# A linear-attention layer and a top-2 expert layer in one kernel: a new order of the attention's work on four engines

## The chip, the cores and the metric

One core of a Trainium2 chip. The metric is device time in microseconds for one launch, the median of several runs; lower is better.

## The reference, cut to what matters

The first half is a recurrence over 768 time steps for 4 x 8 heads with a 40 x 40 state each; the second half routes each of 3072 rows of 320 to two of eight experts.

```python
for t in range(S):                                   # S = 768, D = 40
    y[:, :, t] = np.einsum('bhd,bhde->bhe', rt, state)
    Sa = np.einsum('bhde,bhe->bhd', state, at)
    state_decay = state * wt[:, :, None, :] - np.einsum('bhd,bhe->bhde', Sa, bt)
    state = state_decay + np.einsum('bhd,bhe->bhde', vt, kt)
...
logits = x @ w_gate                                  # x: y as (3072, 320)
noisy_logits = logits + np.log1p(np.exp(x @ w_noise)) * noise
top2 = np.argpartition(-noisy_logits, 2, axis=1)[:, :2]   # weights: softmax of the two
...
h = np.maximum(x[mask] @ w1[e], 0.0)                 # e = 0..7, F = 1024
out[mask] += top2_w[mask, k, None] * (h @ w2[e])
```

## The kernel before

**Units.** The sequence is cut into 12 chunks of 64 steps, and the 32 heads into two halves; a *unit* u (0 to 23) is one chunk of one half, 16 heads, so that u and u+2 are consecutive chunks of the same heads and share the state `S[u%2]`. Inside a unit the recurrence is done with matmuls: decays are multiplied into the inputs, a 64 x 64 triangular system per head is inverted, and the state is carried to the next chunk.

**What is done for a unit.** `scans` (L471) makes the cumulative decays with two scans on VectorE, `B` (L474) and `wq` (L478). `prods` (L479) multiplies them into k, b (`kb`, one GpSimd instruction of 1024 columns, L483) and a (`a`, L484). `LS` (L485) makes the triangular blocks on TensorE and copies them to `lab`. For four units at a time, `xtr` and `xmask` turn the blocks round, `solve` (L503) inverts 32 x 32 triangles column by column (j = 1 to 30, two tensor-tensor operations of j(31-j) elements for each), and `tout` (L510) transposes the result into `rp` and `dg`. `TA` and `TB` (L514, L523) build the 64 x 64 inverses from them. Then, in order: `W2`, `AK`, `U`, `UT`, `KBT`, `W1`, `P`, `dS`, `Y`, `RL` and `ST`, each some 16 to 32 small float32 matmuls (the profile counts each twice) and one copy or product out of PSUM. `P`'s product with the mask is `pm` (L612), `AK`'s is `akm` (L540); `dS` (L580) adds the unit's part to the state in two VectorE operations (L593, L594); `Y` (L613) makes the output, `xT` (L627) scales it; `RL` (L628) brings it back to rows and gives the routing's logits.

**Order.** Everything up to the experts is issued in the order of the program on each engine (`run`, L641). Step n of that loop works on several units at once: Y and RL of n-1, the middle part of n, AK, KBT, W1 and ST of n+1, scans, products and LS of n+8, and the solve for the next group of four units. With q = n mod 4, GpSimd does columns 1 to 13 of the solve in steps q = 0 and 1, VectorE columns 14 to 30 in q = 2, `tout` follows in q = 3, and TA and TB are done for two units at a time in q = 3 and q = 0. PSUM tiles come from a pool of three double banks (`p2`) and one of two banks (`p1`), each in rotation. `warm` (L450) issues matmuls of zeros into a tile ahead of the real ones.

**Routing.** After units 7, 15, 19, 21 and 23 `routed` (L108) runs `route` (L121) as a whole: the gate, the two largest logits, the positions in the experts' lists (with matmuls for running counts). `scatter` (L152) then writes list entries with indirect DMAs from GpSimd, so many in each step (L673), and `turn` (L115) copies the lists once, after unit 19. `zero` (L97) clears the output in steps 8 to 11. **Transfers** of the inputs are issued by the sync engine: `load` (L454) for the unit n+9, `load2` (L464) for n+2.

**Experts.** After the attention, eight experts run one after the other with split float16 matmuls (L277, L291). Their order is made by a planner.

Of the kernel before, what the change touches and what calls it, by code (L numbers as in the profile page):

```python
# [21 lines left out]
NA=20  # L22
# [20 lines left out]
class Moe:  # L43
    def __init__(s,nc,tc,ctx,aps):
        s.nc,s.tc=nc,tc
        s.wgn_d,s.nz_d,s.w1_d,s.w2_d,s.out_d=aps
        ec=ctx.enter_context
        s.kp=ec(tc.tile_pool(name="mk",bufs=1))
        s.rp=ec(tc.tile_pool(name="mr",bufs=MRB))
        s.dp=ec(tc.tile_pool(name="md",bufs=1,space=DRAM))  # L50
        s.scat=[]; s.half=0; s.parts=PARTS; s.cap=CAP; s.rts=list(RTS); s.todo=[]
        s.consts()
# [50 lines left out]
    def logit(s,n):  # L103

        if n==0: s.n0=0
        if n==s.n0: s.lg=s.rp.tile([128,RT,16],F32,name="lg")
        return s.lg[:,n-s.n0]
    def routed(s,n,ps,tag,bufs):  # L108

        if n-s.n0!=s.rts[0]-1: return  # L110
        s.route(s.n0,s.rts.pop(0),ps,tag,bufs)
        if n<NA: s.nc.sync.dma_start(s.xd[1][128*s.n0:128*n+128].rearrange("(p a) f->p (a f)",p=128),s.xd[0][128*s.n0:128*n+128].rearrange("(p a) f->p (a f)",p=128))
        s.n0=n+1
        if n+1==NA: s.turn()
# [6 lines left out]
    def route(s,n0,T,ps,tag,bufs):  # L121
# [4 lines left out]
        oh=s.gate(lg,s.nz[:,n0:n0+T],T,w[:,:,0],w[:,:,1])  # L126
# [3 lines left out]
        cnt=r("cnt",dt=F16); nc.vector.tensor_tensor(cnt,oh[:,:,0],oh[:,:,1],op=ALU.add)  # L130
        pr=ps.tile([128,T,8],F32,name="pr",tag=tag,bufs=bufs)
# [5 lines left out]
        for j in range(T): nc.gpsimd.tensor_tensor(h,p,cnt[:,j],op=ALU.add); p=h  # L137
        s.cumh=h
        rk=r("rk",(1,8))
# [11 lines left out]
        if n0+T>=NA: s.scatter(len(s.todo))  # L151
    def scatter(s,n):  # L152
# [8 lines left out]
    def gate(s,lg,nzt,T,w0,w1):  # L161
# [4 lines left out]
        u=r("u"); nc.scalar.activation(u,zc,AF.Exp)  # L166
        w=r("w"); nc.vector.tensor_scalar(w,u,1.0,None,op0=ALU.add)
        L=r("L_"); nc.scalar.activation(L,w,AF.Ln)
        iv=r("iv"); nc.scalar.activation(iv,L,AF.Exp,scale=-1.0)
        d=r("d"); nc.vector.scalar_tensor_tensor(d,w,1.0,u,op0=ALU.subtract,op1=ALU.subtract)  # L170
# [6 lines left out]
        nc.vector.tensor_tensor(z,z,lg[:,:,0:8],op=ALU.add)  # L177
        l12=r("l12")
# [6 lines left out]
        nc.scalar.activation(q[:,:,1],q[:,:,0],AF.Exp)  # L185
        nc.vector.tensor_scalar(q[:,:,2],q[:,:,1],1.0,1e-9,op0=ALU.add,op1=ALU.add)
# [189 lines left out]
NW,NAB,NKB=LP+3,LP+2,LP+1  # L376
RF=104

# [10 lines left out]
def host_att(inp):  # L389
# [12 lines left out]
            'iw':np.ascontiguousarray(iw.reshape(2,40,256)),'vt':np.ascontiguousarray(v.reshape(NU,2,64,320)),'pad':pad}  # L402

class Att:
    P2=3; P1=2
    def __init__(s,nc,tc,ctx,A,m):
# [10 lines left out]
        s.rb=[t([128,8,64],F32,name=f"rb{i}") for i in range(3)]  # L417
        s.vt=[t([128,8,64],F32,name=f"vt{i}") for i in range(2)]
        s.vu=[t([128,2,8,40],F32,name=f"vu{i}") for i in range(3)]
# [7 lines left out]
        s.tt={}; s.akm={}; s.pm={}; s.W={}; s.ut={}  # L427
# [36 lines left out]
    def load2(s,u):  # L464
        nc=s.nc
        for n,sl in (('gr',s.r),('gv',s.vt),('grb',s.rb)):
            z=s.fl(sl[u%len(sl)]); s.pads(z,u,sl)
            for y in range(2): nc.sync.dma_start(z[64*y:64*y+48],s.A[n][u,y])
        z=s.vu[u%3]
        for b in range(2): s.last=nc.sync.dma_start(z[64*b:64*b+64,b].rearrange("p k d->p (k d)"),s.A['vt'][u,b])  # L470
    def scans(s,u):  # L471
# [6 lines left out]
        V.tensor_tensor_scan(w,w,s.fl(s.d1f)[R],0.0,op0=ALU.mult,op1=ALU.add)  # L478
    def prods(s,u):  # L479
        G=s.nc.gpsimd; R=slice(0,RF); B=s.B[u%2]  # L480
        kb=s.kb[u%NKB][R].rearrange("p j (x t)->p j x t",x=2); a=s.a[u%NAB][R]
        b1=B[R,2:522].rearrange("p (j o c)->p j o c",c=65,o=1)[:,:,:,0:64].to_broadcast([RF,8,2,64])
        G.tensor_tensor(kb,kb,b1,op=ALU.mult)  # L483
        G.tensor_tensor(a,a,s.wq[u%NW][R,:,0:64],op=ALU.mult)  # L484
    def LS(s,u):  # L485
        nc=s.nc; pp=s.p2("ls"); kb,a=s.kb[u%NKB],s.a[u%NAB]; kf=s.fl(kb)
        for hh in range(4):
            for q in range(2):
                for b in range(2):
                    for y in range(2):  # L490
                        Y=slice(64*y,64*y+64); j=2*hh+b; x=128*j+(64 if b==0 else 0)-(0 if q else 32); o=64*b+32*q
                        nc.tensor.matmul(pp[o:o+32,y,64*hh:64*hh+64],a[Y,j,32*q:32*q+32],kf[Y,x:x+64],start=True,stop=True)  # L492
# [10 lines left out]
    def solve(s,eng,js):  # L503
        X=s.X
        for j in js:
# [3 lines left out]
            eng.tensor_tensor(X[:,0:j,j+1:],X[:,0:j,j+1:],t,op=ALU.add)  # L509
    def tout(s):  # L510
        V=s.nc.vector; X=s.X
        V.transpose(s.rp[:,:,32:64].rearrange("p k t->p t k"),X.rearrange("p s t->p t s"))
        for b in range(2): q=slice(64*b,64*b+32); V.transpose(s.dg[q,:,0:32].rearrange("p k s->p s k"),X[q])
    def TA(s,u):  # L514
        nc=s.nc; g,us=divmod(u,4); L=s.lab[g%2]; pp=s.p1t("ta")
# [7 lines left out]
    def TB(s,u):  # L523
# [6 lines left out]
        T=s.tt[u]=s.wk.tile([128,8,64],F32,name="tt",bufs=5)  # L530
        nc.scalar.activation(T.rearrange("p (y h) t->p y (h t)",y=2),pp[:,:,0:256],AF.Copy)
    def AK(s,u):
# [6 lines left out]
        m=s.akm[u]=s.wk.tile([128,8,64],F32,name="akm",bufs=2)  # L539
# [5 lines left out]
    def W1(s,u):  # L545
        nc=s.nc; pp=s.W[u]=s.p2("pw"); v=s.vu[u%3]; first=u<2
        for hh in range(4):
            for y in range(2):
                for b in range(2):
                    r=slice(64*b,64*b+64)  # L550
                    o=64*(b^y); nc.tensor.matmul(pp[o:o+64,y,64*hh:64*hh+40],s.akm[u][r,4*y+hh],v[r,b,4*y+hh],start=hh==0,stop=first,skip_group_check=True)
    def W2(s,u):
        nc=s.nc; pp=s.W[u]; a=s.a[u%NAB]; S=s.S[u%2]
# [7 lines left out]
    def U(s,u):  # L561
# [6 lines left out]
        for b in range(2):  # L568
            o=64*(1-b)
            nc.scalar.activation(s.vu[u%3][o:o+64,b].rearrange("p (y h) d->p y h d",y=2),pp[o:o+64,:,0:256].rearrange("p y (h d)->p y h d",d=64)[...,0:40],AF.Copy,scale=-1.0)  # L570
# [9 lines left out]
    def dS(s,u):  # L580
        nc=s.nc
        if u>=NU-2: return
        pp=s.p1t("ds"); s.warm(pp,1); kt,v=s.kt[u%2],s.vu[u%3]; S=s.S[u%2][:,:,0:40]
        for hh in range(4):
            for b in range(2):
                for y in range(2):
                    j=2*hh+b
                    nc.tensor.matmul(pp[64*y:64*y+64,40*j:40*j+40],kt[:,j,y],v[:,b,4*y+hh],start=True,stop=True)  # L588
        d=pp[:,0:320].rearrange("p (j d)->p j d",d=40)
        gb=s.gam[:,u+2].rearrange("p (j o)->p j o",o=1).to_broadcast([128,8,40])  # L590
        if u<2: nc.vector.tensor_tensor(S,d,gb,op=ALU.mult)
        else:
            nc.vector.tensor_tensor(S,S,d,op=ALU.add)  # L593
            nc.vector.tensor_tensor(S,S,gb,op=ALU.mult)  # L594
    def ST(s,u):
        nc=s.nc
        if u<2: return
        pp=s.p1t("st"); s.warm(pp,1); S=s.S[u%2]
        for hh in range(4): nc.tensor.transpose(pp[:,128*hh:128*hh+128],S[:,2*hh:2*hh+2].rearrange("p b d->p (b d)"),s.m.idm)
        nc.scalar.activation(s.St[u%2][:,:,0:40],pp.rearrange("p (k e)->p k e",e=64)[...,0:40],AF.Copy)  # L600
    def P(s,u):
# [8 lines left out]
        m=s.pm[u]=s.wk.tile([128,2,8,64],F32,name="pm",bufs=1)  # L610
        for y in range(2):
            nc.vector.tensor_tensor(m[:,y],pp[:,y].rearrange("p (j t)->p j t",t=64),s.mk.to_broadcast([128,8,64]),op=ALU.mult)  # L612
    def Y(s,u):  # L613
        nc=s.nc; pp=s.p2("py"); kt,m,r,St=s.kt[u%2],s.pm[u],s.rb[u%3],s.St[u%2]; first=u<2
        if not first:
            for hh in range(4):
                for y in range(2):
                    for b in range(2):
                        r_=slice(64*b,64*b+64)
                        nc.tensor.matmul(pp[64*y:64*y+64,b,64*hh:64*hh+64],St[r_,2*hh+y],r[r_,2*hh+y],start=hh==0,stop=False,skip_group_check=True)  # L620
        for hh in range(4):
            for b in range(2):
                for y in range(2):
                    j=2*hh+b
                    nc.tensor.matmul(pp[64*y:64*y+64,b,64*hh:64*hh+64],kt[:,j,y],m[:,y,j],start=first and hh==0,stop=True,skip_group_check=True)  # L625
        x=s.xt=s.wk.tile([128,8,64],F32,name="xT",bufs=1)
        nc.vector.tensor_tensor(x.rearrange("p (h b) t->p b h t",b=2),pp[:,:,0:256].rearrange("p b (h t)->p b h t",t=64),s.wq[u%NW][:,:,0:64].rearrange("p (h b) t->p b h t",b=2),op=ALU.mult)  # L627
# [178 lines left out]
```

## Time and profile before

| | us |
|---|---|
| three runs | 1111.98, 1115.56, 1115.55 (median 1115.55) |
| the profiled execution | 1110.46 |
| its span from first to last instruction | 1108.7 |
| TensorE busy | 762.4 (69%) |
| VectorE busy | 574.2 (52%) |
| GpSimd busy | 400.8 (36%) |
| ScalarE busy | 298.8 (27%) |
| mean granted TensorE clock | 0.817 of 2.4 GHz |

The busy times are sums over two different stages: attention up to about 677 us, and the experts after it. A share of the whole span therefore says little about either; the stages have to be read one by one. The granted clock is the share of 2.4 GHz that TensorE was allowed (0.5 is its lower level, 1.2 GHz).

### The profile page before, as it was taken

To read this page: it belongs to the slowest core of one execution; us is meant where nothing else is said; L and a number is where in the kernel's file an instruction comes from. 1 tells how busy PE (TensorE), PEld (TensorE's weight loads), DVE (VectorE), ACT (ScalarE), POOL (GpSimd) and SP (SyncE) were. 2 spreads that over 40 slices of the span, in tenths; PEclk is the share of its full clock that TensorE was granted. 3 is DMA by queue.
4 is the path that set the end of the run, shared out by engine and by line. 5 is a ranking of instruction groups with operands and counts; after the bars stand their busy time and mean duration, and the time that the engine had idled before them with its cause. 6 is when DMAs were issued, how large, how long until landed. Compare 5 with 4: busy or idle time off the path is not lost.

```text
span 1108.7 us, 32323 instructions
## 1 busy us (share of the span) xinstructions
PE 762.4 (69%) x14413; PEld 566.2 (51%) x14413; DVE 574.2 (52%) x1043; ACT 298.8 (27%) x587; POOL 400.8 (36%) x543
## 2 busy tenths in 40 slices
PE   1025647754564566656577473399999999999995
PEld 0024646644453455545466363156566676666754
DVE  8376275367535753674064244747566555665231
ACT  0002212211221122112122123325444444444231
POOL 9755314321343154224700301353352433522313
PEclk9996686777667666666586686689999999999998
DMA  6552322242336342112021215634362543622213
GB/s 182 117 159 58 95 66 68 67 122 67 91 82 177 103 112 72 37 36 83 3 69 35 64 42 161 195 89 93 95 166 69 126 93 90 149 46 28 31 14 38
DMA packets 69072, 96.84 MB, mean 87 GB/s; under 512 B 17992, under 2 KB 48668, under 8 KB 68844
## 3 DMA queue, kind: packets, MB, share of 16 engines
q1 hardware_dynamic: 56764, 77.54, 24.9%
q0 software_dynamic: 12160, 17.15, 8.9%
q8 instruction: 115, 1.88, 0.7%
q14 instruction: 33, 0.27, 0.1%
HBM read 76.23 MB, written 21.81 MB: 88 GB/s over the span
## 4 chain that ended last, share of the span: by engine, by line
PE 62%; DVE 18%; POOL 5%; issue 4%; DMA 4%; ACT 3%; SPq 2%; another core or an unknown queue 1%; POOLq 0%; DVEq 0%
PE ph L277 16%; PE po L291 16%; DVE wq L478 4%; DVE X L509 4%; DVE Tt L508 3%; PE tb L529 3%; PE kt L543 3%; PE py L625 3%; PE pp L609 3%; PE u L567 2%; PE ls L492 2%; PE pt L259 2%; PE ta L519 2%; PE ds L588 2%; DVE B L474 2%
## 5 line engine op out<-in xcount | busy, mean ns | idle before, releaser
L492 PE MATMUL ls<-kb,a 64*32 64x64 f32 x1536 | 38.9, 310 | 183.9 <-POOL a L484 153.3
L300 POOL DMA_INDIRECT out_dram<-y,le x48 | 80.1, 1668 | 194.5 <-ACT y L294 191.8
L492 PEld LDWEIGHTS ls<-kb,a 64*32 64x32 f32 x1536 | 28.2, 147 | 192.6 <-POOL a L484 180.7
L279 DVE SCALAR_TENSOR_TENSOR hl<-ph,hh 128x320 f16<-128x320 f32 (+1 forms) x128 | 74.1, 588 | 76.6 <-ACT hh L278 73.9
L277 PEld LDWEIGHTS <-w1h 128*128 128x128 f16 x768 | 74.4, 99 | 57.0 <-issue 5.1
L291 PEld LDWEIGHTS <-hh 128*128 128x128 f16 (+1 forms) x1024 | 84.2, 101 | 35.7 <-issue 3.6
L278 ACT ACTIVATE hh<-ph 128x320 f16<-128x320 f32 (+1 forms) x128 | 65.8, 516 | 130.8 <-PE ph L277 109.6
L627 DVE TENSOR_TENSOR xT<-py,wq 128x512 f32<-128x512 f32 x24 | 16.5, 689 | 157.4 <-PE py L625 151.3
L477 POOL COPY gam<-B 104x8 f32<-104x8 f32 x24 | 6.7, 278 | 224.8 <-DVE B L474 191.5
L612 DVE TENSOR_TENSOR pm<-pp,mk 128x512 f32<-128x512 f32 x48 | 30.9, 686 | 95.9 <-PE pp L609 95.9
L494 ACT ACTIVATE lab<-ls 128x512 f32<-128x512 f32 x24 | 14.3, 597 | 224.0 <-PE ls L492 224.0
L291 PE MATMUL po<-w2h,hh 128*128 128x320 f16 (+1 forms) x512 | 73.5, 284 | 0.0
L246 POOL DMA_INDIRECT xr<-xd,le x56 | 53.8, 961 | 42.7 <-issue 14.6
L277 PE MATMUL ph<-xh,w1h 128*128 128x512 f16 (+1 forms) x256 | 67.6, 347 | 1.7 <-issue 1.2
L291 PE MATMUL po<-w2h,hl 128*128 128x320 f16 (+1 forms) x512 | 68.6, 282 | 0.0
L291 PE MATMUL po<-w2l,hh 128*128 128x320 f16 (+1 forms) x512 | 68.0, 282 | 0.2 <-issue 0.2
L478 DVE TENSOR_TENSOR_SCAN wq<-wq,d1f 104x520 f32<-104x520 f32 x24 | 67.0, 2793 | 0.8
L277 PE MATMUL ph<-xh,w1l 128*128 128x512 f16 (+1 forms) x256 | 66.4, 341 | 0.4 <-issue 0.4
L277 PE MATMUL ph<-xl,w1h 128*128 128x512 f16 (+1 forms) x256 | 66.5, 340 | 0.0
L529 PE MATMUL tb<-rp,dg 64*64 64x64 f32 x768 | 36.8, 319 | 27.9 <-ACT rp L522 23.2
L205 DVE TENSOR_REDUCE yc<-y 128x1 f32<-128x320 f32 (+1 forms) x56 | 25.2, 460 | 58.9 <-ACT y L294 52.5
L156 POOL DMA_INDIRECT ls<-ent,po x48 | 47.4, 987 | 18.7 <-issue 8.1
(218 smaller groups left out, 1726.2 us busy)
## 6 DMA issues: line engine op xcount, KB each, us to landing
w2r<-in_w_dram SPq DMA_DIRECT2D x8, 1280.0 KB
kb<-in_gkb_dram SPq DMA_DIRECT2D x48, 192.0 KB
w1r<-in_w_dram SPq DMA_DIRECT2D x8, 1024.0 KB
wq<-in_gw_dram SPq DMA_DIRECT2D x48, 130.0 KB
a<-in_ga_dram SPq DMA_DIRECT2D x48, 96.0 KB
r<-in_gr_dram SPq DMA_DIRECT2D x48, 96.0 KB
vt<-in_gv_dram SPq DMA_DIRECT2D x48, 96.0 KB
rb<-in_grb_dram SPq DMA_DIRECT2D x48, 96.0 KB
```

The lines of the kernel that those rows point to most:

```text
L156: st=nc.gpsimd.indirect_dma_start(out=s.ls[s.half],out_offset=OFFS(ap=po[:,j,k:k+1],axis=0),in_=s.ent[:,j,k],in_offset=None)
L246: for k in range(c,c+a): nc.gpsimd.indirect_dma_start(out=x[:p,k],out_offset=None,in_=s.xd[w],in_offset=OFFS(ap=li[:p,k,0:1],axis=0))
L277: for i,(a,b) in enumerate(mm): nc.tensor.matmul(ph[:,:n],a,b,start=i==0,stop=i==7)
L278: nc.scalar.activation(hh[:,f],ph[:,:n],AF.Relu)
L279: nc.vector.scalar_tensor_tensor(hl[:,f],ph[:,:n],0.0,hh[:,f],op0=ALU.max,op1=ALU.subtract)
L291: for j in range(c): nc.tensor.matmul(po[p*j:p*j+p,:d],h[:,f,r],w[:,f,d*j:d*j+d],start=k==0,stop=k==23)
L300: st=nc.gpsimd.indirect_dma_start(out=o_,out_offset=OFFS(ap=ix,axis=0),in_=yv,in_offset=None,compute_op=ALU.add)
L478: V.tensor_tensor_scan(w,w,s.fl(s.d1f)[R],0.0,op0=ALU.mult,op1=ALU.add)
L492: nc.tensor.matmul(pp[o:o+32,y,64*hh:64*hh+64],a[Y,j,32*q:32*q+32],kf[Y,x:x+64],start=True,stop=True)
L508: eng.tensor_tensor(t,X[:,j:j+1,j+1:].to_broadcast([128,j,m]),X[:,0:j,j:j+1].to_broadcast([128,j,m]),op=ALU.mult)
L509: eng.tensor_tensor(X[:,0:j,j+1:],X[:,0:j,j+1:],t,op=ALU.add)
L529: nc.tensor.matmul(pp[o:o+64,y,64*hh:64*hh+64],s.dg[r,k],s.rp[r,k],start=True,stop=True)
```

## The change

- **LS one step later.** GpSimd's products are cut in three: `aprod`, and `kprod` for each half of `kb` (x=1: the b half, x=0: the k half). `aprod(n+8)` and `kprod(n+8,1)` stand in step n, `kprod(n+7,0)` at the head of the next one, and `LS(n+7)` is done in step n from products of step n-1. LS reads 32 columns twice instead of 32 columns of the neighbouring half. `kprod` is *held*: x=1 until the reduce of RL (`hl`), x=0 until the last solve operation of the step before (`hA`).
- **The solve on VectorE alone,** in six pieces over four steps by `PLAN`: a piece B ahead of RL's reduce and a piece A after `pm`. `xtr` and `xmask` come in q = 0. `tout` transposes X whole into `dg` too, and GpSimd clears the lower halves.
- **No dS.** `pm` becomes 104 columns wide per head: 64 of P's product and 40 of v and U (copied there by ScalarE, `vc` and `U`). Y's products with `kt` then give the output and the unit's part of the state at once; two identity matmuls add the old S, and one VectorE operation writes the new one.
- **TA and TB** for one unit in each step. Warming matmuls: three ahead of TA and two ahead of ST, none ahead of dS.
- **Routing in parts.** `route` and `gate` become generators of seven pieces; `rstep` runs one at the end of a step, `rdrain` what is left of one before the next begins. The running count is a reduce and an add on VectorE in place of T adds on GpSimd. `turn` is called at the end of the routing that reaches unit 19. Scatters come in two portions a step.
- **Loads.** v is one transfer into `v`, without a copy for each half of U; `rb` has two buffers and is loaded by `load3` after KBT.

```diff
@@ routed, route, gate
-        s.route(s.n0,s.rts.pop(0),ps,tag,bufs)
+        s.rdrain(); s.rg=s.route(s.n0,s.rts.pop(0),ps,tag,bufs)
...
-        if n+1==NA: s.turn()
+    def rstep(s):
+        if s.rg is not None and next(s.rg,0)==0: s.rg=None
+    def rdrain(s):
+        while s.rg is not None: s.rstep()
...
-        for j in range(T): nc.gpsimd.tensor_tensor(h,p,cnt[:,j],op=ALU.add); p=h
+        cr=s.rp.tile([128,8],F16,name="cumr")
+        with nc.allow_low_precision("counts of up to 2048"): nc.vector.tensor_reduce(cr,cnt.rearrange("p t e->p e t"),axis=AX.X,op=ALU.add)
+        nc.vector.tensor_tensor(h,p,cr,op=ALU.add)
@@ Att
+PLAN={0:dict(A=range(1,8)),1:dict(B=range(8,11),A=range(11,15)),2:dict(B=range(15,19),A=range(19,25)),3:dict(B=range(25,31))}
+FT,FS=3,2
...
-    def prods(s,u):
...
-        G.tensor_tensor(kb,kb,b1,op=ALU.mult)
-        G.tensor_tensor(a,a,s.wq[u%NW][R,:,0:64],op=ALU.mult)
+    def aprod(s,u):
+        R=slice(0,RF); a=s.a[u%NAB][R]
+        s.nc.gpsimd.tensor_tensor(a,a,s.wq[u%NW][R,:,0:64],op=ALU.mult)
+    def kprod(s,u,x,e=None):
+        R=slice(0,RF); o=64*x
+        z=s.fl(s.kb[u%NKB])[R]; st=192 if x==0 else 64
+        z=bass.AP(z.tensor,z.offset+o,[z.ap[0],[256,4],[st,2],[1,64]])
+        b1=s.B[u%2][R,2:522].rearrange("p (h b c)->p h b c",c=65,b=2)[...,0:64]
+        s.after(s.nc.gpsimd.tensor_tensor(z,z,b1,op=ALU.mult),e)
@@ tout
+        V.transpose(s.dg[:,:,0:32].rearrange("p k s->p s k"),X)
         V.transpose(s.rp[:,:,32:64].rearrange("p k t->p t k"),X.rearrange("p s t->p t s"))
-        for b in range(2): q=slice(64*b,64*b+32); V.transpose(s.dg[q,:,0:32].rearrange("p k s->p s k"),X[q])
+        for b in range(2): s.nc.gpsimd.memset(s.dg[64*b+32:64*b+64,:,0:32],0.0)
@@ Y
+            if not last:
+                for b in range(2):
+                    nc.tensor.matmul(pp[:,b,0:416].rearrange("p (h x)->p h x",x=104)[...,64:104],s.m.idm,S.rearrange("p (h b) d->p b h d",b=2)[:,b,:,0:40],start=False,stop=False,skip_group_check=True)
+        n=64 if last else 104
...
-                    nc.tensor.matmul(pp[64*y:64*y+64,b,64*hh:64*hh+64],kt[:,j,y],m[:,y,j],start=first and hh==0,stop=True,skip_group_check=True)
+                    nc.tensor.matmul(pp[64*y:64*y+64,b,104*hh:104*hh+n],kt[:,j,y],m[:,y,j,0:n],start=first and hh==0,stop=True,skip_group_check=True)
...
+            nc.vector.tensor_tensor(S.rearrange("p (h b) d->p b h d",b=2)[...,0:40],pv[...,64:104],gb,op=ALU.mult)
@@ run, the body of the loop
+            if ok(n+LP-1): s.kprod(n+LP-1,0,s.hA)
             if ok(n-1): s.Y(n-1)
-            if ok(n): s.W2(n)
+            if ok(n): s.W2(n); s.TA(n)
+            if ok(n+LP-1): s.LS(n+LP-1)
+            if ok(n): s.TB(n)
+            if ok(n+LP): s.scans(n+LP); s.aprod(n+LP)
             if ok(n+1): s.AK(n+1)
             if ok(n): s.U(n); s.UT(n)
-            if ok(n+1): s.KBT(n+1); s.W1(n+1)
+            if ok(n+1): s.KBT(n+1)
+            if n>=8: m.scatter(1 if n<16 else 3)
+            if ok(n+1): s.load3(n+1)
+            if solving and q==0: s.xtr(g+1); s.xmask()
+            sv('B')
+            if ok(n-1): s.RL(n-1)
+            if ok(n+LP): s.kprod(n+LP,1,s.hl if ok(n-1) else None)
+            if ok(n+1): s.W1(n+1)
             if ok(n): s.P(n)
             if ok(n+2): s.load2(n+2)
-            if solving and q<2: s.solve(G,pj[2*q+1])
-            if ok(n): s.dS(n)
-            if ok(n-1): s.RL(n-1)
-            if ok(n+LP): s.scans(n+LP); s.prods(n+LP)
-            if ok(n+LP): s.LS(n+LP)
-            if solving and q==2: s.solve(V,range(J1,31))
+            if ok(n+1): s.vc(n+1)
+            s.hs=None
+            sv('A'); s.hA=s.hs
             if solving and q==3: s.tout()
...
             if ok(n+1): s.ST(n+1)
-            if n>=8: m.scatter(2 if n<16 else 5)
+            m.rstep()
+            if n>=8: m.scatter(1 if n<16 else 2)
```

## Rows read from the trace of the kernel before

**Rows 1.** Windows by stage; columns: stretch, its length, engines' busy us, PEclk, DMA, GB/s.

```profile
98.00:506.00 408.00, 250.57 (x7780) 211.41 (x7780) 218.43 (x358) 85.36 (x178) 135.81 (x213) 0.70 0.31 84
506.00:677.00 171.00, 107.58 (x3122) 90.76 (x3122) 61.81 (x204) 36.44 (x84) 40.52 (x84) 0.72 0.16 49
677.00:1108.70 431.70, 383.68 (x2772) 246.48 (x2767) 230.44 (x407) 167.21 (x309) 154.89 (x126) 0.95 0.41 95
```

**Rows 2.** Timeline of GpSimd, one step: start, duration, line, out<-in, [idle <-releaser].

```profile
437.39 2.17 POOL L483 TENSOR_TENSOR kb<-kb,B 104x1024 f32<-104x1024 f32 x1
...
440.73 1.17 POOL L484 TENSOR_TENSOR a<-a,wq 104x512 f32<-104x512 f32 x1 [1.18 <-DVE wq L478]
```

**Rows 3.** Timeline of VectorE around the same step.

```profile
432.40 1.29 DVE L612 TENSOR_TENSOR pm<-pp,mk 128x512 f32<-128x512 f32 x2 [3.17 <-PE pp L609]
...
437.44 3.21 DVE L478 TENSOR_TENSOR_SCAN wq<-wq,d1f 104x520 f32<-104x520 f32 x1
...
449.69 0.69 DVE L627 TENSOR_TENSOR xT<-py,wq 128x512 f32<-128x512 f32 x1 [9.04 <-PE py L625]
...
456.37 0.49 DVE L593 TENSOR_TENSOR S<-S,ds 128x320 f32<-128x320 f32 x1
...
457.69 1.23 DVE L474 TENSOR_TENSOR_SCAN B<-wq,d 104x520 f32<-104x520 f32 x1
```

**Rows 4.** Timeline of TensorE around the same step.

```profile
429.65 1.09 PE L543 MATMUL kt<-idm,kb 128*128 128x128 f32 x8
...
441.96 1.08 PE L492 MATMUL ls<-kb,a 64*32 64x64 f32 x46 [6.76 <-POOL a L484]
```

**Rows 5.** Timeline of VectorE, one run of the solve, columns 14 to 30.

```profile
358.77 1.26 DVE L509 TENSOR_TENSOR X<-X,Tt 128x238 f32<-128x238 f32 x1
...
360.07 0.41 DVE L508 TENSOR_TENSOR Tt<-X 128x240 f32<-128x240 f32 x1
...
361.83 0.41 DVE L508 TENSOR_TENSOR Tt<-X 128x238 f32<-128x238 f32 x1
...
363.59 0.40 DVE L508 TENSOR_TENSOR Tt<-X 128x228 f32<-128x228 f32 x1
...
365.29 0.38 DVE L508 TENSOR_TENSOR Tt<-X 128x210 f32<-128x210 f32 x1
...
368.42 0.32 DVE L508 TENSOR_TENSOR Tt<-X 128x150 f32<-128x150 f32 x1
...
371.70 0.21 DVE L509 TENSOR_TENSOR X<-X,Tt 128x30 f32<-128x30 f32 x1
```

**Rows 6.** Timeline of VectorE, the first unit's second scan.

```profile
10.28 1.24 DVE L478 TENSOR_TENSOR_SCAN wq<-wq,d1f 104x520 f32<-104x520 f32 x1
```

**Rows 7.** Timeline of TensorE in a later step.

```profile
556.92 0.39 PE L452 MATMUL ds<-d 128*128 128x512 f16 x1
...
558.30 0.69 PE L634 MATMUL rl<-iw,xT 64*64 64x64 f32 x32
...
560.31 1.15 PE L625 MATMUL py<-pm,kt 128*64 128x64 f32 x32
```

**Rows 8.** Timeline of VectorE, a transpose of X.

```profile
386.49 1.94 DVE L512 STREAM_TRANSPOSE rp<-X 128x1024 f32<-128x1024 f32 x1
```

**Rows 9.** Windows of two single steps, columns as in rows 1.

```profile
436.00:458.00 22.00, 14.00 (x430) 11.52 (x430) 8.75 (x12) 3.96 (x8) 5.71 (x7) 0.69 0.28 79
...
643.00:655.00 12.00, 11.10 (x419) 9.39 (x415) 3.94 (x7) 3.36 (x7) 0.00 (x0) 1.00 0.27 81
```

**Rows 10.** Timeline of TensorE, a routing's first matmul and a late `tb`.

```profile
520.08 0.21 PE L132 MATMUL pr<-cnt,tri 128*128 128x64 f16 x1 [7.97 <-DVE cnt L130]
...
632.94 1.53 PE L529 MATMUL tb<-rp,dg 64*64 64x64 f32 x32 [8.06 <-ACT rp L522]
```

**Rows 11.** Timelines of GpSimd and TensorE, the first solve and the first U.

```profile
44.37 0.24 POOL L508 TENSOR_TENSOR Tt<-X 128x30 f32<-128x30 f32 x1
...
98.03 1.13 PE L567 MATMUL u<-w,tt 64*64 64x64 f32 x32 [0.18 <-ACT w L560]
```

## Prediction before the change was run

> **What bounds the kernel now.** I read the windows view by stage first, then the timelines of GpSimd, VectorE and TensorE through one step, then the same engines where they don't disturb each other. By stage [rows 1]: attention's first sixteen units take 408 us, its last eight 171, the experts 432 of a span of 1108.7. In the experts' stage TensorE is busy 384 of 432 us at a granted clock of 0.95, and the change leaves that stage alone. In the 408 us no engine is busy for more than 251, and the granted clock is 0.70, so here a chain sets the time. It is to be seen in one step [rows 2 to 4]: the scan `wq` on VectorE (3.21 us), then GpSimd's product `a` (1.17, it waited for that scan), then `ls` on TensorE, which idled 6.76 us until `a` was there, then all later matmuls of the step in TensorE's order, and `xT`, for which VectorE idled 9.04 us. The engines take turns: 408/16 = 25.5 us a step. Four steps also hold one solve, 17 of its columns on VectorE in one run of 13.5 us (from 358.36, one operation ahead of the first of [rows 5], to 371.91), with TensorE waiting behind it.
>
> **The change, step by step.** All prices are from one execution of 1110.46 us; the median of the three runs is 1115.55, 1.0046 of it.
>
> *`ls` a step later.* LS(n+7) uses products that were made in the step before. The 6.76 us of idle TensorE go, and so does the chain through GpSimd. What is late next is VectorE, which gets the whole solve.
>
> *The scan without GpSimd beside it.* `wq` took 3.21 us with the product `kb` (2.17 us) started 0.05 us before it [rows 2, 3], and 1.24 with GpSimd on other work [rows 6]. The halves of `kb` are now held until the last solve operation and until the reduce, where VectorE works on PSUM. I take 1.24. Two leftovers: `a` still starts as the scan ends and held one solve operation to 1.26 instead of 0.41 [rows 5]; as `akm` runs first I charge 0.55 a step. The first half product (half of 2.17, as long as `a`) begins beside S and xT (1.2 us) and may hold the scan `B` for 0.15.
>
> *The solve, all on VectorE.* A column costs the same as its mirror (j and 31-j have equal sizes). From the starts in [rows 5], to the last operation's end at 371.91: columns 15 to 18 take 3.52, 19 to 24 4.83, 25 to 30 3.49; 11 to 14, mirrored by 17 to 20, 3.46; 1 to 10, mirrored by 21 to 30, 6.62, of which I give 4.2 to 1 to 7 and 2.4 to 8 to 10 by their sizes. Together 21.9 us in four steps, where VectorE had 13.5 in one.
>
> *`dS` goes, the output product carries the state.* The matmuls of dS and its warming (1.4 us of TensorE at full clock, from ds to rl in [rows 7]) and one of two S operations (0.49, [rows 3]) go. Y's products with `pm` get 104 columns for 64: at most 40/64 more of the 1.15 us that they last, 0.7, and nothing if loading weights bounds them; with two identity products I take 0.7 in all, between 0.3 and 1.4. ScalarE, busy 85 of 408 us [rows 1], copies v in time that it has; without that cover U's own copies would come that much later. Warming rises from two matmuls a step to five, at most 0.39 us each [rows 7], in TensorE's waits; without these it would add 1.2.
>
> *The new loop,* from the end of one masking `pm` to that of the next, on VectorE [rows 3, 6]: piece A (or the two transposes), S 0.49 and xT 0.69 with their gaps 1.25, scans 1.23 and 1.24 with the reciprocal between them 2.75, the 0.15 above, akm (size of xT) 0.7, then the longer of two tails, then pm 1.3. One tail is TensorE's from kt to pm, 2.75 (kt at 429.65, pm at 432.40, [rows 3, 4]), plus RL's 0.6 [rows 7], 3.35 us; the other is piece B with 0.55 and a reduce of 0.3. Fixed: 6.15. With a transpose of 1.94 [rows 8] for each of rp and dg:
> q=0: 3.9+6.15+3.35 = 13.4; q=1: 4.2+6.15+3.35 = 13.7; q=2: 3.46+6.15+4.37 = 14.0; q=3: 4.83+6.15+4.34 = 15.3. Four steps 56.4, sixteen 226 us.
> TensorE's own sum at full clock is shorter: a step of 419 matmuls took 11.10 us of a 12 us step at 1.00 [rows 9], 26.5 ns each; a new step has about 470, 12.5 us. At the lower level they would take up to twice that, 25.
>
> *Routing in parts.* It held TensorE 7.97 us at once [rows 10]; now it is some 8 us of VectorE in seven pieces, behind piece A: 8 us on the loop of steps 8 to 14. *Clock:* two of sixteen steps at the lower level (first ones, and where a routing part leaves TensorE idle), at 23 for 14 us, 18 more. So 226+8+18 = 252 for 408: **156 us gained.** Bounds: no cold step 174, eight cold ones 102.
>
> *Before the first unit.* The solve started on GpSimd at 44.4, after the setup of the routing, and U(0) ran at 98.0 [rows 11]. Now no solve operation stands on GpSimd; with the mask behind that setup I take X at 41 us, and VectorE needs 21.9 of solve, three pairs of scans at 2.75, 3.9 of transposes and 3 of other work to 78; TA, TB and the copies bring U(0) to 84. **14 us gained,** 0 to 18: if the sync queue brings the loads later, nothing.
>
> *Units 16 to 23.* No scans: while the solve lasts, four loops less their scans (56.4 - 4*2.9 = 44.8) and 2 for routing pieces, 47; after it TensorE's own order, 12.5 less LS (64 of 470 matmuls, 1.7) and 0.4 for waits on copies, four times 11.2, 45. Routing drains stand in the path at n=20, 22 and 24 (4+6+5). Scatters stay a cost: eight in a row held TensorE's `tb` for 8.06 us [rows 10]; fourteen now come together at n=22, and 3+2 in other steps. I take 26 for all of that and 5 for the last unit. 138 for 171: **33 us gained,** 15 to 50.
>
> *Queues.* On sync, `rb` is loaded after Y's release and v is one transfer, so 14 issues a step, some 7 us of 14; the loads move 1.7 MB a step, 122 GB/s at 14 us, against 95 in the experts' stage at a share of 0.41, so they fit. On GpSimd the held products stand in front of gam, a and the scatters; gam is needed a unit later, a in the next step.
>
> **Sum:** 1110.5 - 156 - 14 - 33 = 907.5; times 1.0046, **912 us.**
>
> **Rivals.**
> *A. The clock stays mixed.* TensorE waits in each loop for akm and pm (1 to 2 us), and a step with a long wait ran at 0.69 [rows 9]. With a mean near 0.75 a step takes about 18 instead of 14.7, and the last eight 3 more each: 912+53+24, about 990, up to 1005. Against it: the step at 1.00 was idle for 0.9 of 12 us too, and a slow TensorE fills its own gaps. [...]
> *B. The change doesn't free `ls`.* If order is kept by whole tiles, LS waits for the product that is now held behind piece A: at most 2 us a step, 32 in all, 945. For it: the product stands just ahead of LS in the code. Against it: LS now reads only the other half.
> *C. Slower: VectorE is locked out.* Each of the solve's 360 operations that meets a GpSimd product costs 0.85 us more (1.26 against 0.41, [rows 5]). If all did: 912+306, about 1218. It decides from 240 operations on. Against it: products last 3.4 us a step and are held beside PSUM work; only the first operation was hit before.
> *D. Nothing:* the chain moves into GpSimd's waits and the step stays at 25: about 1115.
>
> **How the numbers follow.** A measurement of this kernel can tell 0.5% from no change. The forecast has 0.70 (870 to 960), A 0.17, B 0.07, C 0.03, D 0.03. Faster 0.94, within 0.5% 0.02, slower 0.04. The low end takes out the cold steps and gives the two other terms their best (873, so 872); the high end reaches through A, 1005.
>
> **What would show it.** Right: `wq` near 1.24; `ls` without an idle of 6 us before it; `xT` or S starting straight after the last solve operation; four steps of 56 to 65 us; a granted clock above 0.85 in the sixteen units; U(0) near 84. Wrong: solve operations of over 1 us in rows (C), `ls` released by GpSimd (B), granted clock near 0.7 with TensorE busy all step (A), GpSimd's last half product ending after the next step has begun.

## The result, and the profile after the change

The changed kernel takes 946.26 us (median of four runs, 943.62 to 947.05) where the kernel before takes 1113.76 on the same chip: a ratio of 0.849, 95% interval 0.847 to 0.852. The profiled execution took 946.22, its span is 944.5.

The windows by stage of the changed kernel, cut as in [rows 1] (from the first U to the seventeenth, from there to the last `xT`, the rest), and below them one stretch of 20.2 us inside the second stage:

```profile
87.50:343.60 256.10, 213.19 (x7377) 177.62 (x7373) 208.83 (x443) 99.83 (x210) 79.11 (x91) 0.93 0.48 132
343.60:508.70 165.10, 114.69 (x3040) 91.52 (x3040) 65.84 (x230) 43.10 (x100) 43.37 (x82) 0.78 0.19 51
508.70:944.50 435.80, 385.46 (x2767) 247.11 (x2767) 230.72 (x409) 167.44 (x309) 156.67 (x128) 0.94 0.41 94
...
423.20:443.40 20.20, 8.89 (x93) 5.99 (x90) 0.99 (x3) 0.67 (x2) 17.37 (x32) 0.68 0.18 41
```

The first sixteen units fell from 408 to 256 us, and the granted clock there rose from 0.70 to 0.93. The first U runs at 87.5 instead of 98. The last eight units went from 171 only to 165 us, and the rest from 431.7 to 435.8. Together: 10.5 + 151.9 + 5.9 - 4.1 = 164.2, the difference of the two spans. 162.4 of it were gained in the first sixteen units and ahead of them.

Of the 151.9 us of the first sixteen units, 114.5 were idle time of TensorE (its idle time is a stretch less its busy time) and 37.4 its busy time, for 403 matmuls fewer and at the higher clock. The largest of its waits in the kernel before, 98 to 506 us (in all, times, longest):

```profile
PE ls L492 <- POOL a L484: 102.5, 15, 7.8
```

The changed kernel has no such wait from its first U to its seventeenth.

One step, timeline of VectorE, for [rows 3]:

```profile
171.33 0.68 DVE L654 TENSOR_TENSOR xT<-py,wq 128x512 f32<-128x512 f32 x1
171.93 1.23 DVE L496 TENSOR_TENSOR_SCAN B<-wq,d 104x520 f32<-104x520 f32 x1
...
173.44 1.24 DVE L500 TENSOR_TENSOR_SCAN wq<-wq,d1f 104x520 f32<-104x520 f32 x1
...
175.59 0.68 DVE L536 TENSOR_TENSOR Tt<-X 128x240 f32<-128x240 f32 x1
```

The same step on GpSimd, for [rows 2], and the first and last of the sixteen scatters in a row that fill the stretch of 20.2 us:

```profile
170.29 1.19 POOL L511 TENSOR_TENSOR kb<-kb,B 104x512 f32<-104x512 f32 x1 [3.94 <-DVE X L537]
...
174.81 1.19 POOL L505 TENSOR_TENSOR a<-a,wq 104x512 f32<-104x512 f32 x1 [1.40 <-DMA kb<-in_gkb_dram]
...
423.18 1.00 POOL L164 DMA_INDIRECT ls<-ent,po  x1 [13.14 <-DVE po L156]
...
442.46 0.96 POOL L164 DMA_INDIRECT ls<-ent,po  x1 [0.19 <-issue]
```

TensorE in the step, for [rows 4], and in that stretch:

```profile
172.81 0.86 PE L520 MATMUL ls<-kb,a 64*32 64x64 f32 x64
...
425.95 0.42 PE L648 MATMUL py<-pm,kt 128*64 128x104 f32 x4 [0.24 <-issue]
...
434.56 0.46 PE L589 MATMUL pw<-S,a 64*64 64x64 f32 x3 [0.46 <-issue]
435.98 0.26 PE L589 MATMUL pw<-S,a 64*64 64x64 f32 x1 [0.95 <-issue]
...
444.50 0.26 PE L589 MATMUL pw<-S,a 64*64 64x64 f32 x1 [1.05 <-issue]
445.89 0.70 PE L589 MATMUL pw<-S,a 64*64 64x64 f32 x11 [1.13 <-issue]
446.52 1.46 PE L472 MATMUL ta<-d 128*128 128x512 f16 x3
```

In the step, `wq` takes 1.24 us, `ls` follows without idle time, and `a` is off the path (it starts as `wq` ends, though its line names a transfer). In the stretch, every gap on TensorE is put down to "issue": it waits for nothing that the profile shows, and yet it starts one to five matmuls and then pauses for 0.2 to 1.1 us, 93 matmuls in 20.2 us. It recovers some 2 us after the last scatter. The same is to be seen at 349 to 361 (ten scatters) and 475 to 487 us (eight). Those three stretches stand in steps of 31.7, 34.2 and 27.6 us from `xT` to `xT`, where most steps around them take 13 to 16.

The other engines also hear from TensorE late. In the stretch the last products of `py` on TensorE, and S on VectorE, which waits for TensorE's semaphore alone (a semaphore is the counter by which one engine tells another that it is done):

```profile
430.28 0.40 PE L648 MATMUL py<-pm,kt 128*64 128x104 f32 x3 [0.47 <-issue]
...
445.99 0.49 DVE L653 TENSOR_TENSOR S<-py,gam 128x320 f32<-128x320 f32 x1 [21.80 <-remote]
```

Here "remote" means that the profile has no instruction that ended just before the wait did. Fifteen us lie between the two. The wait of [rows 10] was of this kind already: in the kernel before, `tb` waited for ScalarE's copy `rp`, and `rp` started only after the last of the eight scatters (issued from 621.1 to 631.0 us), 7.6 us after the products that it copies.

```profile
624.55 0.33 PE L519 MATMUL ta<-rp,lab 32*32 32x32 f32 x4 [0.38 <-issue]
...
632.51 0.77 ACT L522 ACTIVATE rp<-ta 32x256 f32<-32x256 f32 x2 [7.32 <-remote]
```

Whether the products or only the signals were late the profile does not tell, since it models the ends of matmuls.

### The profile page after: what moved, and what is told of

It is laid out like the page before. It is cut to its first block, busy times and chain, and to the rows that moved or that the text cites. A ratio compares the mean times of both kernels' runs of the same rounds, so it can differ in the third digit from the quotient of the medians.

```text
span 944.5 us, 31363 instructions
## 1 busy us (share of the span) xinstructions
PE 732.4 (78%) x13861; PEld 531.6 (56%) x13861; DVE 570.4 (60%) x1183; ACT 319.7 (34%) x635; POOL 343.1 (36%) x399
## 3 DMA queue, kind: packets, MB, share of 16 engines
q0 software_dynamic: 12160, 17.15, 10.5%
## 4 chain that ended last, share of the span: by engine, by line
PE 65%; DVE 16%; issue 8%; DMA 3%; SPq 3%; POOL 3%; ACT 2%; another core or an unknown queue 0%; ACTq 0%; DVEq 0%; POOLq 0%
PE ph L294 19%; PE po L308 18%; PE pp L628 3%; DVE X L537 3%; DVE Tt L536 3%; PE kt L572 3%; PE py L648 2%; PE pt L276 2%; PE tb L558 2%; PE rl L661 2%; PE u L597 2%; DVE pm L631 2%; PE ut L607 1%; PE pw L589 1%; PE pw L580 1%
## 5 line engine op out<-in xcount | busy, mean ns | idle before, releaser
L511 POOL TENSOR_TENSOR kb<-kb,B 104x512 f32<-104x512 f32 x48 | 63.7, 1330 | 122.4 <-DVE X L537 68.2
L536 DVE TENSOR_TENSOR Tt<-X 128x30 f32<-128x30 f32 (+9 forms) x180 | 68.4, 380 | 10.6 <-POOL X L529 5.6
L520 PE MATMUL ls<-kb,a 64*32 64x64 f32 x1536 | 25.4, 253 | 56.2 <-POOL kb L511 51.6
L537 DVE TENSOR_TENSOR X<-X,Tt 128x30 f32<-128x30 f32 (+9 forms) x180 | 63.5, 353 | 6.6
L222 DVE TENSOR_REDUCE yc<-y 128x1 f32<-128x320 f32 (+1 forms) x56 | 25.2, 460 | 56.4 <-ACT y L311 52.9
L311 ACT ACTIVATE y<-po,le 128x320 f32<-128x320 f32 (+1 forms) x56 | 28.2, 505 | 88.8 <-PE po L308 85.6
L520 PEld LDWEIGHTS ls<-kb,a 64*32 64x32 f32 x1536 | 20.5, 119 | 58.8 <-POOL kb L511 57.1
L308 PEld LDWEIGHTS <-hl 128*128 128x128 f16 (+1 forms) x512 | 42.4, 101 | 14.7
```

Source lines behind the costliest of these rows:

```text
L308: for j in range(c): nc.tensor.matmul(po[p*j:p*j+p,:d],h[:,f,r],w[:,f,d*j:d*j+d],start=k==0,stop=k==23)
L511: s.after(s.nc.gpsimd.tensor_tensor(z,z,b1,op=ALU.mult),e)
L536: eng.tensor_tensor(t,X[:,j:j+1,j+1:].to_broadcast([128,j,m]),X[:,0:j,j:j+1].to_broadcast([128,j,m]),op=ALU.mult)
L537: s.hs=eng.tensor_tensor(X[:,0:j,j+1:],X[:,0:j,j+1:],t,op=ALU.add)
```

## The experiments

They were made on three chips. I name an occasion by what the kernel before took on it: 1070, 1112, 1111.

**Occasion 1070: are the starved stretches the scatters' or the copies' doing?** Two bulk copies between the row tables are issued in the same steps as two of the bursts.

Without scatters (all 48 left out):

```diff
 def scatter(s,n):
...
-    for j,k in s.todo[:n]:
-        st=nc.gpsimd.indirect_dma_start(out=s.ls[s.half],out_offset=OFFS(ap=po[:,j,k:k+1],axis=0),in_=s.ent[:,j,k],in_offset=None)
...
     s.todo=s.todo[n:]
```

> Left out: all 48 scatters of list entries, so the experts gather the default row and add nothing of use; one magnitude test reads another tile. Theory S (GpSimd's scatters, sixteen or ten or eight in a row, hold up TensorE's issue at 349-361, 423-446 and 478-487 us of the changed kernel): the three stalls go, about 11 + 20 + 9 us; units 16 to 23 (xT of unit 15 to xT of unit 23) fall from 171 to 125-138, the whole from 946 to 900-915. Theory C (the copies of rows, 1.3 and 0.6 MB, issued at 352.8 and 421.0 hold it): the stalls stay, units 16 to 23 at 163-171, the whole 935-946.

Rows written twice, no copies:

```diff
 def rows(s,n,xt):
-    s.nc.sync.dma_start(s.xd[n>=NA][128*n:128*n+128],xt)
+    for i in range(n>=NA,2): s.nc.sync.dma_start(s.xd[i][128*n:128*n+128],xt)
...
 def routed(s,n,ps,tag,bufs):
...
-    if n<NA: s.nc.sync.dma_start(s.xd[1][128*s.n0:128*n+128].rearrange("(p a) f->p (a f)",p=128),s.xd[0][128*s.n0:128*n+128].rearrange("(p a) f->p (a f)",p=128))
```

> Each unit's rows are written to both row tables as they come (160 KB more each step), and the three copies from table to table go. Theory S: the stalls at the scatters stay, only the issue gaps of the steps around 217-246 us (3.7 + 1.4 + 1.0) shrink: 938-946. Theory C: the stalls of 349-361 and 423-446 go: 910-925.

Scatters held to places in the step:

```diff
 if ok(n-1):
     s.Y(n-1)
+    if n>=16: m.scatter(1,s.hx)
...
-if n>=8: m.scatter(1 if n<16 else 3)
+if n>=15: m.scatter(1,s.hu)
+if n>=16: m.rstep()
...
-if n>=8: m.scatter(1 if n<16 else 2)
+if n>=14: m.scatter(1,s.hpm)
```

with the same line after AK (`s.hk`) and RL (`s.hl`), one more `m.rstep()` after P, and `turn` called just before the first list entry that follows it. The scatters that came in one go at the end of a routing are taken out; what is left over follows the loop's last steps. So the edit changes two things, the places of the scatters and the pace of the routing. A scatter so called also waits for the instruction named: `hx` is xT, `hk` akm, `hu` ScalarE's copy of ut, `hl` the reduce of the logits, `hpm` pm.

> Nothing left out. Each scatter waits for one place in the step (xT, akm, the ut copy, the logits, pm), so that at most five lie in a step, some 3 us apart; routing of units 8 to 23 gets three parts a step instead of one. Theory S, with the two lone scatters at 321.2 and 327.7 us of the changed kernel, which left no gap on TensorE: units 16 to 23 at 125-140, the whole 905-918. Rival N (each scatter costs TensorE its 1.3 us wherever it stands): units 16 to 23 at 160-171, the whole 936-948. Theory C: as N.

The solve in one run:

```diff
-PLAN={0:dict(A=range(1,8)),1:dict(B=range(8,11),A=range(11,15)),2:dict(B=range(15,19),A=range(19,25)),3:dict(B=range(25,31))}
+PLAN={0:{},1:{},2:dict(A=range(1,31)),3:{}}
```

> The 30 columns of a solve again in one run, in the third step of four, all on VectorE; the other three steps have none. Theory P (a piece must fit beside a step; VectorE holds xT and S of its step behind the run of some 24 us): that step takes 30-35 us, the others 11-13 each (TensorE's chain), four steps 66-74 instead of 59.7: the whole 970-1005. Rival V (only the sum of VectorE's work counts, 50.6 of 59.7 us either way): four steps 58-62, the whole 940-955.

Measured against 1069.65: without scatters 890.6 (ratio 0.832, 0.829 to 0.834), rows twice 895.4 (0.835, 0.832 to 0.838), scatters held 877.8 (0.820, 0.816 to 0.824), solve in one run 973.2 (0.909, 0.907 to 0.912). From the `xT` of unit 15 to that of unit 23 the first three take 124.1, 123.6 and 110.5 us. All three totals lie below every range that was set for them: the ranges were set from 946 us, where the kernel before takes 1114. Leaving out the scatters and leaving out the copies seemed to do the same, which neither theory allows. The solve in one run tells more: it has both the bursts and the copies, and its TensorE goes on. Windows of its burst of sixteen scatters, and S in it, which no longer waits for a late signal:

```profile
482.50:502.70 20.20, 18.92 (x562) 15.01 (x556) 5.92 (x12) 7.10 (x17) 17.32 (x32) 0.96 0.38 88
...
487.57 0.49 DVE L653 TENSOR_TENSOR S<-py,gam 128x320 f32<-128x320 f32 x1 [3.18 <-PE py L648]
```

562 matmuls in the time in which the changed kernel got 93. On this chip there was nothing to remove, and theory S and theory C are both unproved here. What the held scatters gain over no scatters at all (12.8 us) goes with the routing in three parts a step: TensorE's waits for its counts (`pr`) in units 16 to 23 are 3.7 us instead of 12.5.

The solve in one run did what theory P said, at a higher price: its steps from 170.94 on take 13.9, 33.2, 12.8 and 14.6 us, 74.7 for four (the sums are of the unrounded starts), against 58.2 for four in the rows-twice run of the same occasion. That the whole lies in theory P's range of 970 to 1005 is luck: the range was 24 to 59 us above 946, and the run took some 78 more than the rows-twice run. Its timeline of TensorE shows the wait, behind 21 us of solve on VectorE:

```profile
218.92 1.13 PE L661 MATMUL rl<-iw,xT 64*64 64x64 f32 x32 [11.81 <-DVE xT L654]
```

**Occasion 1112: the chip, and the products.** A new theory, K, had to be tried: the starving belongs to some chips.

> The changed kernel itself, once more, since in the solve-in-one-run experiment (bursts of ten, sixteen and eight scatters and the copies of rows as in the changed kernel) TensorE showed no starved stretch in units 16 to 23, and the kernel before took 1070 us there and not 1114. Theory K (the starving during scatters belongs to the chip or the occasion, not to the program alone): where the kernel before takes some 1070 us, units 16 to 23 take 125-140 us and the whole 898-912; where it takes some 1114, 163-171 and 940-948. Theory S (it belongs to the program): 163-171 and a ratio of 0.847-0.852 anywhere.

> The kernel before, once more, for its profile. Theory K: where it takes some 1070 us, the last eight units' stretch (506 to 677 us of its first profile, 171 us) is shorter by 10-30 us, because TensorE goes on during its bursts of eleven and eight scatters; the first sixteen units (408 us) change by under 2%. Rival G (the granted clock differs between the two occasions all over): both stretches shrink by the same 4%.

> The held scatters (at most five in a step, routing of units 8 to 23 in three parts a step), beside the changed kernel on the same chip. Theory K, on an occasion without starved stretches: what is gained is only the waits of TensorE for the routing drained in one go (pr at 420.8 and 473.3, 2.1 + 5.1 us, and the last scatters): 8-20 us less than the changed kernel. Theory S: 30-40 us less.

The changed kernel took 948.8 (ratio 0.851, 0.846 to 0.856), with the three starved stretches again, and the held scatters 897.5 (0.807, 0.802 to 0.811): 51 us less, more than the 30 to 40 of theory S. Windows of the last eight units, first of the changed kernel, then of the one with held scatters:

```profile
344.60:514.30 169.70, 120.34 (x3040) 95.71 (x3040) 66.05 (x231) 43.17 (x100) 43.51 (x82) 0.74 0.17 50
```

```profile
342.10:470.40 128.30, 101.72 (x3042) 84.09 (x3040) 65.83 (x230) 43.67 (x101) 43.20 (x79) 0.89 0.24 65
```

41 of the 53 us between the two spans are here, with the same scatters and copies; 9 lie behind the last `xT` (435.5 to 426.6), and these are not the bursts': on occasion 1070 the held scatters gain the same 9 there on the rows-twice run (434.5 to 425.4). In the 41, TensorE's gaps put down to "issue" fell from 26.7 to 6.7 us, its waits for the counts from 12.4 to 3.6, and its busy time by 18.6, with the clock at 0.89 instead of 0.74; other waits grew by some 6. The copies were kept, so theory C falls, and the gaps go with the bursts: theory S holds on such a chip. That the routing's new pace is not what removes them is shown below by the run with routing at once. Theories K and S forecast the same where the kernel before takes some 1114, so K rests on occasion 1070.

The stage of the held scatters on occasion 1070, the same kernel:

```profile
342.20:449.40 107.20, 89.98 (x3040) 74.67 (x3040) 65.64 (x230) 42.99 (x100) 43.46 (x81) 0.98 0.28 77
```

The first sixteen units take 255 us on both chips. So 21 us of the stage are left that only the starving chip shows: even held apart, the scatters seem not to be free there.

The kernel before took 1114.6 and its stretch of 506 to 677 us is 171.3 again; its TensorE starves in its own burst of eleven scatters (539.5 to 552.3):

```profile
539.19 0.69 PE L559 MATMUL pw<-S,a 64*64 64x64 f32 x32
539.71 0.71 PE L538 MATMUL ak<-a,kb 64*64 64x64 f32 x19
540.83 0.35 PE L538 MATMUL ak<-a,kb 64*64 64x64 f32 x5 [0.41 <-issue]
...
553.19 0.26 PE L567 MATMUL u<-w,tt 64*64 64x64 f32 x1 [1.06 <-issue]
```

**The key products free.**

```diff
-if ok(n+LP-1): s.kprod(n+LP-1,0,s.hA)
+if ok(n+LP-1): s.kprod(n+LP-1,0)
...
-if ok(n+LP): s.kprod(n+LP,1,s.hl if ok(n-1) else None)
+if ok(n+LP): s.kprod(n+LP,1)
```

> GpSimd's two key products wait for no VectorE instruction any more (each starts as soon as its data is there). Theory L (VectorE's scans and products wait for the port while GpSimd's two-input products run: the second scan 1.24 us alone, 3.21 beside one in the kernel before): wq again 2-3.3 us in most steps, the first solve product or akm no longer held, 1-2 us more in each of 24 steps, the whole 15-40 us more than the changed kernel. Rival W (the waits themselves cost as much, since TensorE's LS comes a step later anyway): within 5 us of it.

It took 950.5 (0.854, 0.850 to 0.859) beside 948.8: no difference that this can tell. `wq` stayed at 1.24 us, since `a` stands ahead of the half products on GpSimd and itself waits for `wq`. The collision moved into the solve. Groups by line on VectorE from 157 to 340 us, first the changed kernel, then free products:

```profile
L536 DVE TENSOR_TENSOR Tt<-X 128x184 f32<-128x184 f32 (+14 forms) x83 | 32.3, 389 | 2.3
L537 DVE TENSOR_TENSOR X<-X,Tt 128x168 f32<-128x168 f32 (+14 forms) x84 | 28.3, 337 | 3.0
...
L631 DVE TENSOR_TENSOR pm<-pp,mk 128x512 f32<-128x512 f32 x22 | 14.2, 686 | 10.0 <-PE pp L628 10.0
...
L665 DVE TENSOR_REDUCE lg<-rl 128x16 f32<-128x128 f32 x11 | 3.2, 288 | 12.8 <-ACT xr L664 12.8
```

```profile
L536 DVE TENSOR_TENSOR Tt<-X 128x130 f32<-128x130 f32 (+14 forms) x86 | 42.6, 495 | 2.4
L537 DVE TENSOR_TENSOR X<-X,Tt 128x108 f32<-128x108 f32 (+14 forms) x87 | 35.4, 407 | 3.1
...
L631 DVE TENSOR_TENSOR pm<-pp,mk 128x512 f32<-128x512 f32 x22 | 14.2, 685 | 6.2 <-PE pp L628 6.2
...
L665 DVE TENSOR_REDUCE lg<-rl 128x16 f32<-128x128 f32 x11 | 3.2, 287 | 5.9 <-ACT xr L664 5.9
```

The solve's operations cost 78.0 us instead of 60.6 (six more of them fall in the window, some 2 us), and the two waits lost 3.8 + 6.9 us. Theory L is right on the engine and wrong on the time: VectorE had slack for it, and rival W came true. GpSimd's two half products and two solve operations of one size, one beside them and one after:

```profile
164.22 2.53 POOL L511 TENSOR_TENSOR kb<-kb,B 104x512 f32<-104x512 f32 x2
...
165.74 1.23 DVE L536 TENSOR_TENSOR Tt<-X 128x198 f32<-128x198 f32 x1
167.01 0.36 DVE L537 TENSOR_TENSOR X<-X,Tt 128x198 f32<-128x198 f32 x1
```

The Trainium skill (SBUF — State Buffer, Who interferes with whom) has it that a VectorE instruction with two inputs in SBUF contends with a GpSimd instruction that reads SBUF; the trace agrees, 1.23 us instead of 0.36.

**Occasion 1111: the best version, routing, warming.**

> The changed kernel, a third time, to stand beside the other three of this call. Theory K (the starving during bursts of scatters belongs to some chips and not to others): where the kernel before takes some 1070 us, no starved stretch, units 16 to 23 at 125-140 us and the whole 898-912; where it takes some 1112, starved stretches and 943-952, as on the first two occasions.

> The held scatters and the rows written twice together. From the two alone (held: 898 where the kernel before takes 1112, 878 where it takes 1070; the issue gaps at the copies some 4-6 us): 888-897 on the one kind of chip, 868-877 on the other. Rival: 160 KB more in each of twenty steps meets the loads of the next units, and gives back 5 us or more.

Routing at once, on top of that version:

```diff
-s.rdrain(); s.rg=s.route(s.n0,s.rts.pop(0),ps,tag,bufs)
+s.rg=s.route(s.n0,s.rts.pop(0),ps,tag,bufs); s.rdrain()
```

> As the run with held scatters and rows written twice, but each routing is done whole where it falls due, as in the kernel before, instead of in parts. Theory: TensorE waits for its counts (pr) at units 8, 16 and 20 with the 7.97 us of the kernel before for eight units and 4-5 for four and two: 15-25 us more than that run. Rival V (only VectorE's sum counts): within 5 us of it.

No warming, on the changed kernel:

```diff
-FT,FS=3,2
+FT,FS=0,0
```

> The changed kernel without the five idle products (FT, FS at 0) that TensorE does in each step for nothing; the results do not use them. Theory H (they hold the granted clock at 0.93 in the sixteen units, where the kernel before has 0.70): the clock there falls to 0.70-0.85, each step takes 1-2 us more, the whole 10-35 us more than the changed kernel. Rival: the steps are dense enough without; the clock stays over 0.88 and the step is shorter by the 1.2 us of the five, the whole 10-30 us less.

The changed kernel: 947.2 (0.852, 0.850 to 0.855), starved as before. Held scatters with rows written twice: 895.8 (0.807, 0.805 to 0.809), no better than held scatters alone on the occasion before (0.807): as far as two chips can be compared, the copies cost nothing that shows in the end. Routing at once on top of it: 922.6 (0.830, 0.826 to 0.834), 27 us more, a little over the 15 to 25 forecast. It is still 24.6 us below the changed kernel, with the routing in larger pieces than there: that much at least is not the routing's pace but the scatters' places (the copies are gone there too, which by itself showed nothing). The wait is the one expected; from the matmul's line in that kernel, what TensorE waited for ahead of `pr`:

```profile
L135 PE MATMUL pr<-cnt,tri x5: 173/209/221, 218.1 to 518.6; 128*128 128x64 f16 x2, 128*128 128x16 f16 x2, 128*128 128x32 f16 x1
its engine sat idle before it (us, times) until:
  DVE cnt L132: 30.6, 4
```

With the parts it is one wait of 3.6 us. No warming: 942.6 (0.847, 0.843 to 0.851), whose interval meets that of the changed kernel. Its first sixteen units, then the same stretch of the changed kernel (first U to `xT` of unit 15):

```profile
87.50:341.20 253.70, 203.91 (x7146) 179.25 (x7143) 208.73 (x442) 98.14 (x206) 73.63 (x83) 0.87 0.48 133
```

```profile
87.50:335.90 248.40, 210.26 (x7227) 176.16 (x7225) 208.29 (x443) 98.07 (x206) 73.75 (x83) 0.92 0.48 136
```

The clock is at 0.92 with the idle products and 0.87 without. The stretch is 253.7 us without them and 248.4 to 250.9 with them (three profiles of the changed kernel): 3 to 5 us. Over the whole kernel nothing is left of it that these runs can tell. Both theories put too much on it.

## Why the prediction was right, and where it failed

**Right, by its own steps.** The time (912 forecast, 946 measured) lies in the forecast's own range of 870 to 960. The chain was the right one: TensorE's 102.5 us of waiting for `a` are gone, `ls` waits no more, `wq` takes 1.24, `xT` and S follow the solve's last operation or TensorE's output within 0.8 us, the clock is above 0.85. The first sixteen units were put at 252 us and took 256. The solve in pieces is worth 16 us in four steps by the experiment. Of the drains the prediction kept 4 + 6 + 5, and TensorE waited 2.1 + 5.1 + 5.2 for their counts.

The sum gave 907.5 us for the profiled execution, which took 946.2. Of the 38.7 us between them, 27.1 are in units 16 to 23 and some 4 in each of the three other places (first U, first sixteen units, experts), all to the same side. The range was wide enough to hold that.

**Terms that were a little off.** Four steps (`xT` from 157.85 to 217.52) took 59.7 us for 56.4. Gaps on TensorE of the kind "issue" explain most: of the gaps over 0.5 us there are five in that stretch, 5.2 us together, and over the first sixteen units such idle adds up to some 26 us in 16 steps, where the kernel before had some 8. They are on occasion 1070 too (24.6 without any scatter), so they are not the scatters'; the prediction had no term for them. Y's products with 104 columns take 1.65 us and the identity products about 0.7 more, so 1.2 in all for the 0.7 taken, inside its bounds. U(0) came at 87.5 for 84: ahead of it GpSimd's products still meet the scans, which take 1.79 us instead of 1.24. The price of holding the products was right in rows and idle in the sum: without the hold the time is the same.

**The step that failed: units 16 to 23.** "33 us gained, 15 to 50" was 5.9. The stage was put at 47 + 45 + 5 for the engines' own work, 15 for the drains and 26 for the scatters, 138 in all; it took 165.1. The term that was mis-sized is "I take 26 for all of that", the scatters. On occasion 1070 the stage takes 120.5 without any scatter, where the other terms say 112: so some 8 us are theirs, and the scatters took some 45 instead of 26, an estimate across two chips. Their count was right; their grouping was not. The prediction spread them as the program issues them, three and two in a step and fourteen at n=22. But once the products end, nothing ties GpSimd to the step: it runs ahead to its next wait for `po`, and then issues what has piled up, ten, sixteen and eight in a row, since the routing of units 8 to 15 is finished only by the drain at n=20. And a burst costs TensorE more than [rows 10] showed: eight scatters made `tb` late by 8.06 us there, and in the burst of sixteen the 93 matmuls of 20.2 us would have been 2.5 at the prediction's 26.5 ns each, so some 18 were lost. Held apart, with the routing in smaller parts, the same scatters left the stage at 128.3 us on a chip of the starving kind.

**The rivals.** A (mixed clock) did not come: 0.93 in the sixteen units. In the starved stage the clock was 0.74 to 0.78 and rose to 0.89 with the gaps removed, so there it followed the gaps. B: `ls` was free. C: in two steps of three one operation is held, to 0.7 to 1.1 us, and the free products showed that more than twice as many would still cost nothing. D fell.

**Open.** Why TensorE starves is not shown. On chips where the kernel before takes 1111 to 1114 it did each time; on the one where it takes 1070 no kernel that ran did, with the same bursts. Neither the changed kernel itself nor a profile of the kernel before is on record for that chip. The transfers are not what fills the stretch: the DMA share in it is 0.18. The Trainium skill (Runtime: NRT & Kernel Launch, Instruction fetch mechanics) has it that each engine's sequencer fetches the next block of 256 instructions over a DMA queue of its own while it executes the current one, at a cost "mostly hidden". The gaps here come after every one to five matmuls and not once in 256 instructions, so the page does not describe them; a late fetch would also not explain why VectorE hears of finished products 15 us late. No run here tells the causes apart.

One rival was not tried: the recording. Every run listed in these experiments has its span and clock on record, so each was recorded. Of the held-scatter kernel's updates of VectorE's semaphore in the experts' stage, where GpSimd issues indirect DMAs too, the trace of occasion 1070 holds all 377 and that of occasion 1112 only 345; in the first sixteen units both hold all 405. Records go missing on the chip that starves, in stages with indirect DMAs. A recording that can't keep up may be what holds TensorE, or may suffer from the same cause; nothing here shows how much an unrecorded run would starve.

## What to carry to other kernels

Look at how an engine's free work is paced once its other work ends: indirect DMAs that a program issues evenly leave in one burst if only data holds them, and where the kernel before takes 1111 to 1114 a burst of sixteen cost TensorE some 18 of its 20 us. Holding each of them to an instruction of the step it belongs to, and cutting the routing into three parts a step, took the changed kernel from 947-949 to 896-898 us there, the best ratio of the versions that ran (0.807). And compare variants on one chip: two edits looked like a cure on a chip that did not have the illness.

## What the runs showed of the hardware

TensorE starts 93 matmuls in 20.2 us while GpSimd issues sixteen indirect DMAs 1.27 us apart on one chip, and 562 in the same time on another; in the first case VectorE starts 15 us after the last products that it waits for. Two lone scatters, at 321.2 and 327.7 us of the changed kernel, left no gap on TensorE; yet spread over all steps of units 16 to 23 they left that stage 21 us longer on the one chip than on the other. Two-input solve operations on VectorE took 17 us more beside GpSimd's products, 2 of them for operations more in the window, without lengthening the kernel. Five idle matmuls in each step went with a granted clock of 0.92 instead of 0.87, and moved the time by nothing that could be told.
